# Two decode layers with a cached attention: scores in PSUM, and a larger rest of one key kept between the layers

## The chip, the core and the metric

The kernel runs on one core of a Trainium2 chip. The core has a matrix engine (TensorE, PE in the profile), a vector engine (VectorE, DVE), a scalar engine (ScalarE, ACT), a general engine (GpSimd, POOL) and a queue engine (SyncE, SP), which here only issues transfers. All of them work out of SBUF, a memory with 128 partitions; TensorE writes into a second memory, PSUM, which the kernel divides into tiles of 512 float32 columns. Sixteen DMA engines move data between the chip's main memory and SBUF. The metric is the time of one execution on the device, in microseconds (us).

## The reference

One token for each of two sequences (B = 2) goes through layer A, layer B, and then through both once more with the same weights and the same caches:

```python
def _A_ref(x, k_cache, v_cache, wq, wo):              # B=2, H=32 heads, Sk=8192 keys, Dh=128
    q = (x @ wq).reshape(B, Sq, H, Dh).transpose(0, 2, 1, 3)
    scores = einsum("bhqd,bhkd->bhqk", q, k_cache) * (Dh ** -0.5)
    p = softmax(scores)
    o = einsum("bhqk,bhkd->bhqd", p, v_cache)
    return o.transpose(0, 2, 1, 3).reshape(B, Sq, H * Dh) @ wo

def _B_ref(x, w_gate, w_up, w_down):                  # D=576, Df=4608
    return (gelu(x @ w_gate) * (x @ w_up)) @ w_down

x = A_x
for layer in range(2):
    x = x + _A_ref(layernorm(x), k_cache, v_cache, wq, wo)
    x = x + _B_ref(layernorm(x), w_gate, w_up, w_down)
```

All is float32. The two caches hold 2 x 32 x 8192 x 128 values each, 268 MB, and each layer needs all of both, against some 25 MB in the SBUF tile that the kernel loads into. So nearly all of the caches is read twice.

## The kernel before

**The work in items.** An item is a pair of heads of one sequence, or a single head. There are 30 pairs, and the heads 30 and 31 of the two sequences are four singles, s0 to s3. Layer 0 takes the 30 pairs and then s0, s1, s2, s3; layer 1 goes backward, s3, s2, s1, s0 and then the pairs. The keys of an item are laid out with 128 rows of them over the partitions and the rest along the columns. A part is 16 such rows for every partition, that is 2048 float32 columns (PART) and 1 MiB. A pair has eight parts of K and eight of V, a single four of each.

**One item on the engines.** Per unit of one or two parts, `multiply` (L578) has VectorE multiply the keys with the query, which lies repeated over the partitions in the first 128 columns of the PSUM tile qp[n % 2]; the product goes over the keys in SBUF. GpSimd adds the two halves of each row (L582). `add_up` (L588) then has VectorE sum what is left of each row into S, the scores; it is called one unit later than `multiply`, so that VectorE's order is multiply of unit k+1, sum of unit k. S is a tile of the pool `work`, which has two buffers. `peak`, `highest`, `softmax` and `total` take the maximum (L618, L625), the exponentials on ScalarE (L636, from S into `prz`, of which there are two, one for even and one for odd items) and their sum. `values` (L665) has TensorE multiply the exponentials with V, in 64 matmuls for a pair, into a PSUM tile acc. `invert`, `gather` (L680, L682: four VectorE instructions, each adding to the result of the one before) and `context` finish the item, mostly while the next is at work.

**SBUF as one tile.** `space` is one tile of END columns, and all caches and weights are loaded into it. The class `Space` decides where and when: loads stand in one list in the order of the calls of `cache`, `rows`, `out_rows`, `down` and so on. `pump` issues the first of the list as soon as its columns are free, and never a later one before it. `done` frees the columns of a part after the last instruction that reads it, and pumps again. All loads go to SP's one queue in that order, so a load that waits for its columns holds all later ones. In steady state three regions of eight parts (P0, P1, P2) take turns: the load of V goes out when VectorE has made the last sum over the keys whose place it takes, the load of K when TensorE has done the last matmul on the values whose place it takes.

**Between the layers.** What is left in SBUF at the end of layer 0 need not be read again: `kept` names four parts of K of s3 and s2, two of K of s1, and four parts of V of s1, s2, s3. For kept keys the product may not go over the keys; it goes to a `scratch` place of two parts. The MLP of layer 0 and the projections stream their weights through a ring in the middle, MID to MIDEND.

**Layer 1's start.** Its first items find their keys in SBUF. Their work is a chain on VectorE (the query's copy L604, `multiply`, `add_up`, `held_keys` L610 and L613, `gather`), while SP loads the two missing parts of K of s1, K and V of s0, and then the first pairs in several pieces.

Of the kernel before, what the change touches and what calls it, by code (L numbers as in the profile page):

```python
# [45 lines left out]
END = 24 * PART + 768  # L46
MID = 18 * PART
# [50 lines left out]


@with_exitstack  # L100
def decode_layers(ctx, tc, x_in, kc, vc, wq, wo, wg, wu, wd, out):
# [29 lines left out]
    def cache(kind, layer, item, at, lo=0, hi=None):  # L131
# [6 lines left out]
        def load(a):  # L138
            at_of[base] = a - lo * PART
            nc.sync.dma_start(space[:, a:a + (hi - lo) * PART], src[:, lo * PART:hi * PART])  # L140

        sp.queue.append(([base + (k,) for k in range(lo, hi)], at + lo * PART, (hi - lo) * PART, load))
# [88 lines left out]
    idle = {(1, NT - 2, 0): (512,), (1, NT - 2, 5): (512, 256), (1, NT - 1, 0): (160,)}  # L231
# [13 lines left out]
    scratch(s1.name, P0 + 4 * PART)  # L245
# [4 lines left out]
    cache("v", 0, s2, home[("v",) + s2.name])  # L250
# [33 lines left out]
    for k in range(2, 4):  # L284
        cache("k", 1, s1, home[("k",) + s1.name], k, k + 1)
# [38 lines left out]
    ones = consts.tile([P, P], F32, name="ones")  # L324
    nc.vector.memset(ones, 1.0)
# [11 lines left out]
    eight = consts.tile([P, 2, 4], F32, name="eight")  # L337
# [17 lines left out]
    prz = consts.tile([P, 2, 32, 2, 4], F32, name="prz")  # L355
    nc.vector.memset(prz.rearrange("p n g e r -> p (n g e r)"), 0.0)
# [3 lines left out]
    x10 = consts.tile([P, 16, 10], F32, name="x10")  # L360
# [24 lines left out]
    def turn(first=False):  # L385

        if first:
# [7 lines left out]
        stats = work.tile([P, 6], F32, name="stats")  # L395
        nc.vector.bn_stats(stats, x)
        apart = work.tile([P, B, 4, 6], F32, name="apart")
# [12 lines left out]
    def norm(apart):  # L410
# [3 lines left out]
        mv = work.tile([P, B, 2], F32, name="mv")  # L414
        for b in range(B):
            nc.vector.bn_aggr(mv[:, b, :], every[:, 24 * b:24 * b + 24])
        ve = work.tile([P, B], F32, name="ve")
# [3 lines left out]
        part = work.tile([P, 2, B], F32, name="part")  # L421
# [14 lines left out]
    def attention(layer, items, apart):  # L436
# [121 lines left out]

        def key_of(kind, item, k):
# [6 lines left out]
        def multiply(n, unit):  # L566
            item = items[n]
            lo, hi = unit
            if n not in S:
                S[n] = work.tile([P, 128], F32, name="S")  # L570
# [4 lines left out]
            if layer == 0 and lo < stays("k", item):  # L575
                at = at_of["scratch", item.name] + lo % 2 * PART
# [8 lines left out]
        def add_up(n, unit, half):  # L585
# [6 lines left out]
            n_kept = stays("k", item)  # L592
            if layer == 0 and max(0, n_kept - 2) <= lo < n_kept:
                done(("scratch", item.name, lo % 2))
# [323 lines left out]
```

## Time and profile before

The kernel took 2687.89 us, the median of three runs from 2687.64 to 2688.00 us.

| | profiled execution |
|---|---|
| time of that execution | 2687.68 us |
| its span in the trace | 2685.9 us |
| busy: VectorE | 1876.3 us, 70% |
| busy: GpSimd | 1169.2 us, 44% |
| busy: TensorE matmuls | 941.9 us, 35% |
| busy: ScalarE | 121.2 us, 5% |
| read from main memory | 1152.13 MB, 429 GB/s over the span |
| TensorE's granted clock, mean | 0.628 |

How to read it: the time of an execution is 1.78 us longer than the span, which begins and ends with the first and last recorded instruction. The span falls into stages, and times inside it count from its start: layer 0's pairs from about 30 to 1200 us, its singles to about 1270 us, the projection and the MLP of layer 0 to about 1372 us, layer 1's singles to about 1443 us, layer 1's pairs to about 2606 us, and its MLP to the end. A row of the timeline has start, duration, engine and line, and in brackets how long the engine had been idle and who ended that. Rows marked SPq are transfers being issued, not their time on the way.

### The profile page before, as it was taken

The page shows a single profiled execution, that of the slowest core. Times are in us where ns is not written, and L with a number is a line of the kernel's source. Part 1 is how long each engine was busy: PE and PEld are TensorE (multiplying, and loading weights), DVE is VectorE, ACT ScalarE, POOL GpSimd, SP SyncE. Part 2 cuts the span into 40 slices and gives each one's busy share as a digit, 9 for nine tenths or more (in the row PEclk, how much of TensorE's full clock was granted, in tenths as well). Part 3 has the DMA queues.
Part 4 walks back from the last instruction along what each step waited for, and adds up shares of the span by engine and source line. Part 5 has one row for each costly group of instructions (what it writes and reads, how often), then busy time and mean ns, then how long its engine had stood idle before and what let it go on. Part 6 is the DMA issues. An engine that isn't in the chain of part 4 may idle for free. (4 is left out here: it accounts for less than half of the span.)

```text
span 2685.9 us, 17802 instructions
## 1 busy us (share of the span) xinstructions
PE 941.9 (35%) x7226; PEld 318.8 (12%) x7226; DVE 1876.3 (70%) x1347; ACT 121.2 (5%) x542; POOL 1169.2 (44%) x341
## 2 busy tenths in 40 slices
PE   2322332233233323325764333223323332332345
PEld 0110111011001101102121111001100110110022
DVE  5578777867777787788159877776777778777750
ACT  0000000000000000001000000000000000000000
POOL 2345444544554454455025544554454445444530
PEclk7656665666566566657666666566656656665678
DMA  9999999999999999999999999999999999999998
GB/s 422 436 436 428 432 435 435 435 433 431 433 433 434 433 434 431 433 431 419 406 407 437 435 431 432 433 434 434 431 433 436 433 431 435 435 430 433 432 427 375
DMA packets 38450, 1153.29 MB, mean 429 GB/s; under 512 B 4304, under 2 KB 4960, under 8 KB 16992
## 3 DMA queue, kind: packets, MB, share of 16 engines
q1 hardware_dynamic: 38344, 1152.14, 99.8%
q8 instruction: 57, 0.93, 0.1%
q14 instruction: 25, 0.20, 0.0%
q10 hardware_dynamic: 24, 0.01, 0.0%
HBM read 1152.13 MB, written 0.00 MB: 429 GB/s over the span
## 5 line engine op out<-in xcount | busy, mean ns | idle before, releaser
L582 POOL TENSOR_TENSOR space<-space 128x2048 f32<-128x2048 f32 (+1 forms) x331 | 1165.7, 3530 | 1291.2 <-DVE space L578 1170.3
L578 DVE TENSOR_TENSOR space<-space,qp 128x4096 f32<-128x4096 f32 (+1 forms) x328 | 1126.9, 3451 | 453.9 <-DMA space<-in_A_k_cache_dram 443.5
L588 DVE TENSOR_REDUCE S<-space 128x32 f32<-128x2048 f32 (+1 forms) x331 | 594.4, 1796 | 116.7 <-POOL space L582 113.7
L665 PE MATMUL acc<-space,prz 128*8 128x512 f32 x4096 | 594.0, 743 | 9.7 <-DMA space<-in_A_v_cache_dram 5.0
L693 PE MATMUL spare<-weights,osb 128*64 128x2 f32 (+1 forms) x528 | 70.9, 256 | 1198.9 <-ACT osb L684 1180.2
L693 PEld LDWEIGHTS spare<-weights,osb 128*64 128x64 f32 (+1 forms) x528 | 65.3, 208 | 1215.5 <-ACT osb L684 1195.1
L665 PEld LDWEIGHTS acc<-space,prz 128*8 128x8 f32 x4096 | 113.0, 103 | 425.3 <-issue 419.2
L620 PE MATMUL sm<-ident,m 128*1 128x128 f32 x68 | 24.9, 367 | 335.9 <-DVE m L618 335.9
L684 ACT COPY osb<-osb 128x128 f32<-128x128 f32 x60 | 17.9, 298 | 1764.7 <-DVE osb L682 1764.7
L682 DVE SCALAR_TENSOR_TENSOR osb<-acc,diag,osb 128x128 f32<-128x128 f32 x204 | 71.6, 351 | 7.2
L419 POOL TENSOR_TENSOR rstd<-ve,mhalf 128x2 f32<-128x2 f32 x4 | 2.8, 700 | 164.0 <-DVE ve L418 164.0
L646 PE MATMUL sm<-rs,ones 128*128 128x2 f32 x120 | 35.0, 361 | 77.3 <-ACT prz L636 77.3
L636 ACT ACTIVATE prz<-S,nbs 64x128 f32<-64x128 f32 (+1 forms) x136 | 53.4, 392 | 3.1
L627 PE MATMUL sm<-m,ones 1*128 1x2 f32 (+1 forms) x136 | 39.0, 353 | 23.1 <-DVE m L625 23.1
L620 PEld LDWEIGHTS sm<-ident,m 128*1 128x1 f32 x68 | 5.4, 79 | 347.5 <-DVE m L618 317.6
L625 DVE TENSOR_REDUCE m<-sm 1x2 f32<-1x128 f32 (+1 forms) x68 | 18.9, 278 | 29.7 <-PE sm L620 29.7
L646 PEld LDWEIGHTS sm<-rs,ones 128*128 128x128 f32 x120 | 29.9, 309 | 82.4 <-ACT prz L636 82.4
L802 PE MATMUL acc<-space,xt 128*6 128x288 f32 x256 | 29.2, 568 | 29.2 <-DMA space<-in_B_w_up_dram 14.8
L813 DVE STREAM_TRANSPOSE turned<-acc 128x288 f32<-128x288 f32 x4 | 1.9, 484 | 51.8 <-PE acc L802 51.8
L627 PEld LDWEIGHTS sm<-m,ones 1*128 1x128 f32 x136 | 33.1, 300 | 41.5 <-DVE m L625 41.3
L838 PE MATMUL xps<-space,hT 128*2 128x144 f32 x576 | 32.2, 374 | 15.2 <-DMA space<-in_B_w_down_dram 15.2
L680 DVE TENSOR_SCALAR osb<-acc,diag 128x128 f32<-128x128 f32 x68 | 23.3, 342 | 15.9 <-PE acc L665 15.9
(124 smaller groups left out, 352.7 us busy)
## 6 DMA issues: line engine op xcount, KB each, us to landing
space<-in_A_k_cache_dram SPq DMA_DIRECT2D x8, 4096.0 KB, 24.7
space<-in_A_v_cache_dram SPq DMA_DIRECT2D x4, 4096.0 KB, 30.1
space<-in_B_w_down_dram SPq DMA_DIRECT2D x19, 576.0 KB, 7.3
space<-in_B_w_gate_dram SPq DMA_DIRECT2D x18, 576.0 KB, 7.5
space<-in_B_w_up_dram SPq DMA_DIRECT2D x18, 576.0 KB, 7.8
space<-in_A_wo_dram SPq DMA_DIRECT2D x16, 576.0 KB, 7.5
space<-in_A_wo_dram SPq DMA_DIRECT2D x8, 1152.0 KB, 23.7
space<-in_B_w_gate_dram SPq DMA_DIRECT2D x2, 4608.0 KB, 26.3
```

The lines of the kernel that those rows point to most:

```text
L578: nc.vector.tensor_tensor(out=u, in0=t, in1=qp_of(n)[:, 0:DH].unsqueeze(1).to_broadcast([P, j, DH]), op=ALU.mult)
L582: nc.gpsimd.tensor_tensor(out=half, in0=half, in1=u[:, :, DH // 2:], op=ALU.add)
L588: nc.vector.tensor_reduce(out=S[n][:, 16 * lo:16 * hi], in_=half, axis=AX.X, op=ALU.add)
L620: nc.tensor.transpose(peaks[n], m, ident)
L627: nc.tensor.matmul(low[n], ones[0:1, :], m1, start=True, stop=True)
L636: nc.scalar.activation(prz[rows_, n % 2, 0:item.rows // 4, e, :], s[rows_, 0:item.rows].rearrange("p (g r) -> p g r", r=4), AF.Exp, bias=n ...
L646: nc.tensor.matmul(tot, ones, rs[:, n % 2, :], start=True, stop=True)
L665: nc.tensor.matmul(acc_of(n)[32 * c:32 * c + 8, :], prz[:, n % 2, g, :, :].rearrange("p e r -> p (e r)"), space[:, at:at + 4 * DH], start= ...
L682: nc.vector.scalar_tensor_tensor(t, q[:, r, :], diag[:, r:r + 1], t, op0=ALU.mult, op1=ALU.add)
L693: nc.tensor.matmul(to[:, i, 0:item.heads], t[:, i:item.heads * DH:GH], w, start=True, stop=True,)
L802: nc.tensor.matmul(banks[half][s][32 * c:32 * c + WIN, 0:BF], lhs, space[:, lo:lo + BF], start=key not in done_first, stop=stop,)
L838: nc.tensor.matmul(xps[32 * c:32 * c + B, 0:CW], hT[t // 2][:, t % 2 * NI + i, :], space[:, a:a + CW], start=piece == downs[layer][0] and ...
```

## The change

`END` grows by MORE = 1280 columns, ten of the sixteen rows of a part. With them part 2 of K of s1 keeps its first ten rows between the layers (that is 128 x 1280 float32, 655,360 bytes), and layer 1 loads only the last six, 128 x 768. Room for it comes from smaller work tiles:

- The scores S no longer are a tile of `work` but columns 128 to 255 of the PSUM tile qp[n % 2], whose columns 0 to 127 hold the item's query (for the first item of layer 1 columns 384 to 511 of sm[1], where its query lies in the same tile).
- `prz` is single, the tile of ones [128, 128] becomes a column that is repeated by its access pattern, some small tiles share a buffer or have one buffer in place of two. The idle matmuls between the last `lower` calls are cut into pieces of 256 columns.

Since part 2 of K of s1 is kept in part, its product in layer 0 goes to a scratch place too (`more`, at P2 + 4 PART), and `shorten` then frees all but the ten rows. The scratch of s1 moves from P0 + 4 PART to P0 + 6 PART, and V of s2 in layer 0 is loaded in two halves rather than in one piece.

```diff
+MORE = 10 * DH
-END = 24 * PART + 768
-MID = 18 * PART
+END = 24 * PART + 768 + MORE
+MID = 18 * PART + MORE
...
+    def shorten(self, key, n):
+        lo, hi = self.live[key]
+        self.live[key] = lo, lo + n
+        self.pump()
...
-    def cache(kind, layer, item, at, lo=0, hi=None):
+    def cache(kind, layer, item, at, lo=0, hi=None, skip=0):
...
-            at_of[base] = a - lo * PART
-            nc.sync.dma_start(space[:, a:a + (hi - lo) * PART], src[:, lo * PART:hi * PART])
+            at_of[base] = a - skip - lo * PART
+            nc.sync.dma_start(space[:, a:a + (hi - lo) * PART - skip], src[:, lo * PART + skip:hi * PART])
...
-    idle = {(1, NT - 2, 0): (512,), (1, NT - 2, 5): (512, 256), (1, NT - 1, 0): (160,)}
+    idle = {(1, NT - 2, 0): (256, 256), (1, NT - 2, 5): (256, 256, 256), (1, NT - 1, 0): (160,)}
...
-    scratch(s1.name, P0 + 4 * PART)
+    scratch(s1.name, P0 + 6 * PART)
+    scratch("more", P2 + 4 * PART, 1)
...
-    cache("v", 0, s2, home[("v",) + s2.name])
+    for k in (0, 2):
+        cache("v", 0, s2, home[("v",) + s2.name], k, k + 2)
...
-        cache("k", 1, s1, home[("k",) + s1.name], k, k + 1)
+        cache("k", 1, s1, home[("k",) + s1.name], k, k + 1, MORE if k == 2 else 0)
...
-    prz = consts.tile([P, 2, 32, 2, 4], F32, name="prz")
+    prz = consts.tile([P, 32, 2, 4], F32, name="prz")
...
-        stats = work.tile([P, 6], F32, name="stats")
+        stats = once.tile([P, 6], F32, name="stats")
...
             if n not in S:
-                S[n] = work.tile([P, 128], F32, name="S")
+                bank, at = (sm[1], 3 * DH) if layer == 1 and n == 0 else (qp[n % 2], DH)
+                S[n] = bank[:, at:at + DH]
...
-            if layer == 0 and lo < stays("k", item):
-                at = at_of["scratch", item.name] + lo % 2 * PART
+            if layer == 0 and lo < aside(item):
+                name, k = place_of(item, lo)
+                at = at_of["scratch", name] + k * PART
...
-                if layer == 1 or k >= stays("k", item):
+                some = item is s1 and k == stays("k", item)
+                if some and layer == 0:
+                    sp.shorten(key_of("k", item, k), MORE)
+                elif layer == 1 or k >= stays("k", item):
+                    if some:
+                        sp.free(("k", 0) + item.name + (k,))
                     done(key_of("k", item, k))
...
-                    prz[rows_, n % 2, 0:item.rows // 4, e, :],
+                    prz[rows_, 0:item.rows // 4, e, :],
```

The order in which VectorE, GpSimd and ScalarE get their instructions is the same before and after. What they wait for is not, and SP's list has one load more. In the rows that follow a name ending in _49 is the counter of an engine (or, DMAHW, of a transfer) that the instruction waits for, and 128x32 is the shape of the output.

VectorE, first pair of layer 1, its first units. Here qp_124 (before) and qp_123 (after) are the PSUM tile qp of this item. Before:

```order
L578 TENSOR_TENSOR space<-space,qp_124 128x4096
L588 TENSOR_REDUCE S<-space 128x32 [waits Activation_49,Pool_49]
L578 TENSOR_TENSOR space<-space,qp_124 128x4096 [waits DMAHW1_49]
L588 TENSOR_REDUCE S<-space 128x32 [waits Pool_49]
L654 RECIPROCAL sm_127<-sm_127 128x2 [waits PE_49]
```

After:

```order
L595 TENSOR_TENSOR space<-space,qp_123 128x4096
L605 TENSOR_REDUCE qp_123<-space 128x32 [waits DVE_49,Pool_49]
L595 TENSOR_TENSOR space<-space,qp_123 128x4096 [waits DMAHW2_49,DVE_49]
L605 TENSOR_REDUCE qp_123<-space 128x32 [waits DVE_49,Pool_49]
L676 RECIPROCAL sm_126<-sm_126 128x2 [waits PE_49]
```

The sum now writes the tile that the multiply before it reads, and the multiply behind it reads the tile that the sum wrote; waits are set by tile and not by column, so each of these now waits for VectorE's own instruction ahead of it.

SP, start of layer 1, the loads of keys and values of s1 and s0. Before:

```order
L140 DMA space<-in_A_k_cache_dram 128x2048 [waits DVE_49] x2
L140 DMA space<-in_A_k_cache_dram 128x2048 [waits DMAHW0_49,DVE_49]
L140 DMA space<-in_A_k_cache_dram 128x2048 [waits DMAHW4_49,DMAHW5_49,DMAHW1_49,PE_49]
L140 DMA space<-in_A_k_cache_dram 128x2048 [waits DMAHW2_49]
L140 DMA space<-in_A_k_cache_dram 128x2048 [waits DMAHW3_49]
L140 DMA space<-in_A_v_cache_dram 128x2048 [waits PE_49] x2
```

After:

```order
L146 DMA space<-in_A_k_cache_dram 128x2048 [waits DVE_49] x2
L146 DMA space<-in_A_k_cache_dram 128x2048 [waits DMAHW1_49,DVE_49]
L146 DMA space<-in_A_k_cache_dram 128x768 [waits DMAHW5_49,DMAHW2_49,PE_49]
L146 DMA space<-in_A_k_cache_dram 128x2048 [waits DMAHW6_49,DMAHW3_49,PE_49]
L146 DMA space<-in_A_k_cache_dram 128x2048 [waits DMAHW4_49]
L146 DMA space<-in_A_v_cache_dram 128x2048 [waits PE_49] x2
```

The fourth load is smaller by ten rows; the order is the same.

SP, end of layer 0, the values of s1, s2 and s3. Before:

```order
L140 DMA space<-in_A_v_cache_dram 128x4096 [waits DMAHW5_49,DVE_49]
L140 DMA space<-in_A_v_cache_dram 128x4096 [waits DVE_49]
L140 DMA space<-in_A_v_cache_dram 128x8192 [waits DVE_49,PE_49]
L140 DMA space<-in_A_v_cache_dram 128x4096 [waits DMAHW7_49,PE_49]
L140 DMA space<-in_A_v_cache_dram 128x4096 [waits DMAHW6_49,DVE_49,PE_49]
```

After:

```order
L146 DMA space<-in_A_v_cache_dram 128x4096 [waits DMAHW5_49,DVE_49]
L146 DMA space<-in_A_v_cache_dram 128x4096 [waits DVE_49]
L146 DMA space<-in_A_v_cache_dram 128x4096 [waits PE_49]
L146 DMA space<-in_A_v_cache_dram 128x4096 [waits DVE_49]
L146 DMA space<-in_A_v_cache_dram 128x4096 [waits DMAHW7_49,DMAHW6_49,PE_49]
L146 DMA space<-in_A_v_cache_dram 128x4096 [waits DVE_49,PE_49]
```

The load of 8192 columns, which waited for TensorE and VectorE both, is now two, of which the first waits for TensorE alone.

More of the change, by code (lines that the diff above doesn't have):

```diff
@@ L557, in stays, with aside, place_of @@
             return kept.get((kind,) + item.name, 0)
+        def aside(item):
+            return stays("k", item) + (item is s1)
+        def place_of(item, lo):
+            return ("more", 0) if item is s1 and lo == 2 else (item.name, lo % 2)
         def key_of(kind, item, k):
```

52 lines of the change are left out of this document (28 added, 24 removed).

## The prediction

> **What bounds the kernel now.** I read the page first, for the engine that never rests, then the span cut into its stages, and then the handovers, the places where a load waits for work on an engine.
>
> ```profile
> span 2685.9 us, 17802 instructions
> q1 hardware_dynamic: 38344, 1152.14, 99.8%
> HBM read 1152.13 MB, written 0.00 MB: 429 GB/s over the span
> ```
>
> One queue of loads keeps the DMA engines at work for 99.8% of the span. The stages show where it is slower than it can be (columns: stretch, its length, busy time of PE, its weight loads, DVE, ACT, POOL, TensorE's granted clock, DMA share, GB/s):
>
> ```profile
> 60.00:1160.00 1100.00, 339.57 (x2268) 113.68 (x2268) 806.48 (x506) 49.21 (x224) 510.36 (x141) 0.61 1.00 433
> 1267.00:1283.00 16.00, 12.14 (x183) 5.86 (x183) 2.24 (x8) 1.05 (x5) 0.00 (x0) 0.79 0.95 365
> 1400.00:1470.00 70.00, 34.15 (x199) 11.99 (x198) 67.47 (x62) 3.75 (x19) 41.80 (x15) 0.62 1.02 434
> 1470.00:1480.00 10.00, 3.88 (x17) 1.50 (x21) 5.73 (x6) 1.15 (x5) 2.34 (x1) 0.50 1.00 419
> 1480.00:2560.00 1080.00, 337.92 (x2264) 113.44 (x2260) 801.33 (x504) 49.21 (x224) 509.90 (x140) 0.61 1.00 433
> ```
>
> 433 GB/s is the steady rate: a load of 8 MiB takes 8,388,608 / 433e3 = 19.37 us, a pair 38.7. The rate falls at layer 0's end, 1267 to 1283, and where layer 1's singles hand over to its pairs, 1470 to 1480. There the timeline shows who issues what, and when the keys land (VectorE's idle time ends with the landing):
>
> ```profile
> 1474.11 0.33 SPq L140 DMA_DIRECT2D space<-in_A_v_cache_dram  x1
> 1477.52 4.42 DVE L578 TENSOR_TENSOR space<-space,qp 128x4096 f32<-128x4096 f32 x1 [2.38 <-DMA space<-in_A_k_cache_dram]
> 1507.63 0.33 SPq L140 DMA_DIRECT2D space<-in_A_v_cache_dram  x1
> 1516.85 8.75 DVE L578 TENSOR_TENSOR space<-space,qp 128x4096 f32<-128x4096 f32 x2 [8.17 <-DMA space<-in_A_k_cache_dram]
> ```
>
> The load of V of the first pair goes out at 1474.11, only 3.4 us before the load ahead of it lands at 1477.5. Then V and the next K need 1516.85 - 1477.52 = 39.33 us where two loads take 38.7, so 0.6 us is lost here. One pair later the lead is 1516.85 - 1507.63 = 9.2 us, and VectorE, idle for 8.17 us, is far ahead. So DMA bounds the kernel, except at this handover, where VectorE's chain is nearly too late already.
>
> **The bytes saved.** The load of 128x768 in place of 128x2048 leaves out 128 x 1280 x 4 = 655,360 bytes: at 434 GB/s 1.51 us. Everything behind it in the queue could land 1.5 us earlier, the keys of 1477.52 at 1476.0. That becomes time only if the next load is issued in time. The issue at 1474.11 is SP's, and hangs on VectorE:
>
> ```profile
> SPq L140 <- DVE m L618: 46.7, 4, 22.6
> 1472.86 1.22 DVE L588 TENSOR_REDUCE S<-space 128x16 f32<-128x1024 f32 x1 [1.39 <-POOL space L582]
> DVE S L588 <- POOL space L582: 3.0, 3, 1.4
> DVE space L578 <- ACT osb L604: 2.5, 1, 2.5
> DVE m L625 <- PE sm L620: 0.8, 2, 0.5
> 1378.70 4.49 DVE L578 TENSOR_TENSOR space<-space,sm 128x2048 f32<-128x2048 f32 x2 [2.48 <-ACT osb L604]
> ```
>
> The first row is what SP waited for from 1400 to 1480, the third to fifth are all that VectorE waited for from 1378.6 to 1474.2: GpSimd's sums, the copy of the query before its first multiply, two transposes, and never a transfer. From 1378.70 to the last sum over the pair's keys, which ends at 1474.08, VectorE has one unbroken chain. No landing stands in it, so saved bytes can't shorten it. The query that starts it comes out of the MLP of layer 0, which lies ahead of the smaller load.
>
> **The waits on VectorE.** The edit of S makes a sum and its neighbouring multiplies share a PSUM tile, so VectorE waits for itself. The price, from pairs of rows with and without such a wait:
>
> ```profile
> 1453.15 2.28 DVE L588 TENSOR_REDUCE S<-space 128x32 f32<-128x2048 f32 x1
> 1455.35 4.41 DVE L578 TENSOR_TENSOR space<-space,qp 128x4096 f32<-128x4096 f32 x1
> 1467.02 1.12 DVE L682 SCALAR_TENSOR_TENSOR osb<-acc,diag,osb 128x128 f32<-128x128 f32 x3
> L682 DVE SCALAR_TENSOR_TENSOR osb<-acc,diag,osb 128x128 f32<-128x128 f32 x12 | 4.2, 351 | 0.4
> ```
>
> Without one, the multiply starts 2.20 us after a sum of 2.28: the two overlap by 0.08 us. With one, three instructions of 0.351 that each need the one before take 1.12 us, (1.12 - 3 x 0.351) / 2 = 0.034 us between them. A wait for oneself so costs 0.08 + 0.034 = 0.117 us (with the unrounded times). In the order of the changed kernel I count the rows from the first multiply of layer 1 to 1474 where an added wait is for the instruction directly ahead and no later GpSimd wait covers it: eleven sums and four multiplies, 15 x 0.117 = 1.76 us. Not counted are sums whose query lies in the other tile, and the two that stand ahead of a sum held by GpSimd (of such the 1.39 us above are one).
>
> The Trainium skill says otherwise ("VectorE: DVE Perf Modes", section "The DRAIN you can't avoid"): eight copies with a semaphore after each took the same time as with one after the last, "the semaphore costs nothing extra here". By it this term is nothing. The trace here disagrees, with 0.08 us of overlap where no wait stands and a gap of 0.034 where one does.
>
> **The scores in PSUM.** How much longer a sum takes that writes PSUM has no row; the nearest:
>
> ```profile
> L588 DVE TENSOR_REDUCE S<-space 128x16 f32<-128x1024 f32 x17 | 20.6, 1210 | 3.0 <-POOL space L582 3.0
> L588 DVE TENSOR_REDUCE S<-space 128x32 f32<-128x2048 f32 x3 | 6.8, 2281 | 0.0
> L610 DVE TENSOR_TENSOR qp<-qp,osb 128x512 f32<-128x512 f32 x1 | 0.7, 689 | 0.0
> L613 DVE TENSOR_REDUCE S<-qp 128x4 f32<-128x512 f32 x1 | 0.7, 692 | 0.0
> ```
>
> (2281 - 1210) / 1024 = 1.046 ns an element, so 512 elements would take 1210 - 535 = 675 ns out of SBUF. Out of PSUM they take 692, and into PSUM as well 689. So PSUM adds 0 to 17 ns; below nothing no row points. For 20 sums that is 0 to 0.34 us, of which I take 0.2, nearer the upper end since the two rows agree. VectorE's chain is later by 1.76 + 0.2 = 2.0 us (bounds: 0, if the waits were hidden, to 2.3, with 0.34 for PSUM and two more waits that GpSimd covers in part).
>
> **The sum at the handover.** V then goes out at 1474.1 + 2.0 = 1476.1, and the load ahead of it lands at 1476.0: the queue runs empty. How long a load takes to fill an empty queue, L, I bound from two places. At 1474.11 the lead of 3.4 us lost 0.6, so L is at most 3.4 + 0.6 = 4.0 us. At the program's start
>
> ```profile
> 0.74 0.39 SPq L140 DMA_DIRECT2D space<-in_A_k_cache_dram  x1
> 20.26 4.20 PE L449 MATMUL acc<-space,xt 128*6 128x512 f32 x24 [20.26 <-DMA space<-in_A_wq_dram]
> ```
>
> 4 MiB of K and 3 MiB of wq, 7.34 MB, have landed by 20.26; at 433 GB/s they take 16.95, and 20.26 - 16.95 - 0.74 = 2.6 us, less what of the next load had come in between, so some 2.4. The next keys then land at 1476.1 + L + 38.7 = 1514.8 + L instead of 1516.85: +0.4 us with L = 2.4, +2.0 with 4.0. I take **+1.4**, somewhat above the middle (L = 3.45), since the upper end is from this very handover. All later loads follow at the old spacing, so the shift reaches the end. The saved 1.5 us are in it: without them the load ahead would land at 1477.5, still less than L after the issue at 1476.1, and the result would be the same. The delay on VectorE eats the whole saving.
>
> **The steady pairs.** Per pair three own waits (two sums, one multiply; the others stand ahead of a GpSimd wait) and five writes to PSUM: 0.35 + 0.09 = 0.44 us on VectorE. The issue of V has 9.2 us of lead and needs at most 4.0, so it is covered; the cover ends at 5.2 us. K waits for TensorE, which gets its exponentials 0.44 us later:
>
> ```profile
> 1486.23 0.33 SPq L140 DMA_DIRECT2D space<-in_A_k_cache_dram  x1
> ```
>
> This is the tightest such issue, right behind the handover; V lands a load's 19.4 us after 1477.52, so it has 10.7 us of lead, and 0.44 is nothing beside it. That `prz` is single makes the exponentials wait until the values of the item before are done; those end at 1486 and the next exponentials come after 1507, so 20 us cover it.
>
> **The end of layer 0.** Its singles get 13 such waits, 1.5 us. VectorE there waits for values, and TensorE for the first weights of the projection:
>
> ```profile
> DVE osb L680 <- PE acc L665: 9.3, 3, 7.9
> 1264.35 0.35 DVE L680 TENSOR_SCALAR osb<-acc,diag 128x128 f32<-128x128 f32 x1 [0.89 <-PE acc L665]
> 1270.27 1.14 PE L709 MATMUL xps<-space,oT 128*2 128x144 f32 x16 [1.87 <-DMA space<-in_A_wo_dram]
> ```
>
> Two waits of `gather` for values, of which the last is 0.89 us, and 1.87 us before the projection take up more than 1.5. V of s2 in halves can go out sooner, not later, since its first half no longer waits for VectorE; it costs SP one issue of 0.33 us. So I put this at nothing; if the cover is gone, 1.5 us.
>
> **The end of the program.** The chain of layer 1's last pair is later by the same 0.44 us; its loads of weights wait for it at 2606, in a stretch where the queue is full:
>
> ```profile
> 2600.00:2612.00 12.00, 11.17 (x216) 6.31 (x208) 1.71 (x5) 0.60 (x3) 0.00 (x0) 1.00 1.04 443
> ```
>
> 443 GB/s stand there, so nothing is lost. The shared and single small tiles serve the norms and the MLP, one layer at a time, and the matmuls in pieces of 256 are idle work between loads: nothing for both.
>
> **The sum.** Layer 0 nothing, the handover +1.4, steady pairs and end nothing: 2687.68 + 1.4 = 2689.1 us for the profiled execution, and since the median of the runs is 0.2 above it, 2689.3 us. A difference of 0.2%, 5.4 us, is about what a measurement of this kernel can tell from no change; the forecast lies within it.
>
> **The rivals.**
>
> *The saving survives.* If waits for oneself cost nothing on this chain, VectorE is late by the 0.2 us of PSUM alone, V goes out at 1474.3, and the next keys land at 1474.3 + L + 38.7: with L between 2.4 and 4.0 that is -1.4 to +0.2, with 3.45 -0.4, some 2687.5 us. If VectorE isn't what the handover hangs on at all, the whole 1.5 us come out: 2686.4. For it speaks only that GpSimd's 3.0 us of waits could cover more of the added ones than I counted; against it the row of 1474.11, in which SP waits for VectorE's last sum.
>
> By the rule of the Trainium skill cited above the first half of this case would come about.
>
> *More is lost at the start of layer 1.* The query of the item after next goes into the tile that holds S, so an item's first multiply now hangs on ScalarE's exponentials of two items before. In the singles an item is four multiplies of 2.28 and four sums of 1.21, 14 us of VectorE's chain, so the exponentials are long done. Should they not be, each of the five items ahead of 1474 waits for the 0.5 us between two exponentials, 2.5 us more: +3.9, 2691.8 us.
>
> *The steady pairs lose their cover; slower by far.* Sums now write the tile from which the multiplies read the query for all their 4.41 us. If that made multiplies slower, V of every pair would go out later. A pair has three multiplies of 4.41 and two of 2.28, 17.8 us; the cover of 5.2 us, less the 0.44 already in use, is gone when they take 4.8 / 17.8 = 27% longer. From there each further 0.1 us per pair costs 0.1 x 58 = 5.8 us: slower by over 0.2% from 2693.7 us on, 2717 at 0.5 us. Against it: nothing in the rows above shows a multiply that depends on what else lies in its tile, and VectorE does one instruction after the other but for 0.08 us.
>
> *Faster by over 0.2%.* It needs 5.4 us. The saved 1.5 and all that is missing at 1267 to 1283, 16 x (1 - 365 / 433) = 2.5 us, make 4.0. So there is hardly a way.
>
> **How the numbers follow.** The forecast, saving eaten, from 2688.3 to 2690.2 us with the bounds of L and of VectorE's delay: 0.60. The saving survives, 2686.4 to 2688.1: 0.20. More lost at layer 1's start, 2690.2 to 2692.5: 0.12. Steady pairs slower: 0.06. Much faster: 0.02. The range reaches from 2686.2, the whole saving and 0.2 for the runs' spread, to 2691.2, which takes in the lower half of the third case; outside are about 0.15. The first three cases lie within 0.2% but for a hundredth of the third: within 0.2% 0.91, slower 0.07, faster 0.02.
>
> **What would show it.** In the trace of the changed kernel: sums and multiplies of layer 1's singles start 0.034 us behind the one ahead instead of 0.08 before its end; the first V of the pairs goes out near 1476 with the keys' landing near the same time; the stretch of 1470 to 1480 moves less than 405 GB/s; the distance from that landing to the next but one is over 40 us, against 39.3; the later leads stay near 9 us. It is wrong if V goes out by 1474.5, if the two landings lie under 39.4 us apart, or if a steady pair takes more than 38.8 us.

## The result, and the profile after

The changed kernel takes 2692.18 us (median of 21 runs, 2691.15 to 2693.66), the kernel before 2687.77 us (21 runs, 2686.91 to 2689.08): a ratio of 1.0017 with a 95% interval of 1.0011 to 1.0023. It is 4.4 us slower, within the 0.2% named in the prediction, and 1.0 us above the range, which ended at 2691.2. The profiled execution took 2692.31 us, 1.9 us more than its span.

The page of the changed kernel first: what is read, and who reads it.

```profile
span 2690.4 us, 18204 instructions
q1 hardware_dynamic: 38488, 1151.49, 99.6%
q14 instruction: 29, 0.24, 0.0%
HBM read 1151.47 MB, written 0.00 MB: 428 GB/s over the span
```

0.66 MB less are read, as meant, and yet the span is 4.5 us longer. 402 instructions are new, and the queue named q14 instruction carries 29 packets for 25. Where the queue is slower than before stands in the stretches (columns as in the prediction):

```profile
60.00:1160.00 1100.00, 338.04 (x2268) 113.52 (x2268) 813.85 (x506) 46.86 (x222) 510.01 (x141) 0.61 1.00 433
1267.00:1283.00 16.00, 12.22 (x159) 6.23 (x163) 3.17 (x9) 1.13 (x6) 1.05 (x1) 0.68 0.92 339
1400.00:1470.00 70.00, 33.18 (x193) 12.14 (x193) 65.95 (x58) 3.96 (x22) 40.81 (x15) 0.65 1.02 434
1470.00:1480.00 10.00, 1.56 (x11) 1.13 (x11) 8.10 (x11) 0.15 (x1) 3.39 (x2) 0.50 0.77 308
1480.00:2560.00 1080.00, 341.35 (x2266) 113.45 (x2265) 809.77 (x501) 47.17 (x224) 509.57 (x140) 0.61 1.00 433
```

It is the same two places that were slow before: the end of layer 0 (339 GB/s where 365 stood) and the handover at 1470 to 1480 (308 for 419). The steady pairs run at 433 GB/s as before. The timeline at the handover:

```profile
1379.65 4.49 DVE L595 TENSOR_TENSOR space<-space,sm 128x2048 f32<-128x2048 f32 x2 [1.79 <-ACT osb L626]
1478.33 0.33 SPq L146 DMA_DIRECT2D space<-in_A_v_cache_dram  x1
1521.08 4.42 DVE L595 TENSOR_TENSOR space<-space,qp 128x4096 f32<-128x4096 f32 x1 [10.24 <-DMA space<-in_A_k_cache_dram]
```

The first multiply of layer 1 starts 0.95 us later than before (1378.70). From it to the issue of V take 98.68 us instead of 95.41, 3.27 more. So V goes out 4.22 us later, and the next keys land 4.23 us later. The end of the span, 4.5 us later, adds little: this issue sets the time of all that follows. The load ahead of V, the keys, is issued at 1454.91; its time to landing is

```profile
DMA to landing us min/median/max: 23.1/23.1/23.1
```

so it lands at 1478.0, and the queue is empty when V goes out. From this landing to the next pass 43.1 us, where 39.33 stood. The 1.5 us of saved bytes are nowhere to be seen, and they are gone even ahead of this issue: with them the keys should land at 1476.0, and they land 0.5 us later than before the change (1477.52).

Why VectorE's chain grew by 3.27 us is read from three views of the changed kernel. Its timeline, at a sum between two multiplies and at the multiply with the longest stop ahead of it:

```profile
1423.57 2.29 DVE L595 TENSOR_TENSOR space<-space,qp 128x2048 f32<-128x2048 f32 x1 [0.40 <-issue]
...
1452.43 4.41 DVE L595 TENSOR_TENSOR space<-space,qp 128x4096 f32<-128x4096 f32 x1
1456.94 2.29 DVE L605 TENSOR_REDUCE qp<-space 128x32 f32<-128x2048 f32 x1
1459.27 4.42 DVE L595 TENSOR_TENSOR space<-space,qp 128x4096 f32<-128x4096 f32 x1
```

Its groups by shape between 1379 and 1479 (count, then busy time and the mean ns of one):

```profile
L605 DVE TENSOR_REDUCE qp<-space 128x16 f32<-128x1024 f32 x14 | 17.2, 1227 | 3.4 <-POOL space L599 2.4
L605 DVE TENSOR_REDUCE qp<-space 128x32 f32<-128x2048 f32 x3 | 6.9, 2295 | 0.3
```

Its chain of work, at the sum of 1456.94 (start, length):

```profile
1456.85 0.03 issue
1456.88 0.02 DVEq L605
1456.90 0.04 issue
1456.94 2.31 DVE qp L605
```

The multiply of 1452.43 ends at 1456.84, and the sum starts 0.10 us later; the next multiply follows the sum after 0.04 us. A sum waits for GpSimd already, and in the list of VectorE's instructions its wait for the multiply is an instruction of its own ahead of it: the chain has two pieces of issue there. So a sum's wait costs 0.083 + 0.103 = 0.186 us and a multiply's 0.117. It is not the number of waits that makes the difference: the multiply of 1459.27 waits for a transfer too, as the list of waits ahead of the prediction shows, and still follows after 0.04 us. Eleven sums and four multiplies make 11 x 0.186 + 4 x 0.117 = 2.5 us. A sum that writes PSUM takes 1227 ns for 1210 and 2295 for 2281: 20 of them 0.3 us. And one multiply, which waits for five loads and not for VectorE, starts 0.40 us after the instruction ahead has ended (1423.57); before the change it started 0.04 us before that end (1420.82), so this is 0.44 us more. Together 3.3 us. What makes that multiply stop isn't shown: with the scores alone, or with the same loads and the scores in another tile, it starts within 0.05 us of that end.

### The profile page after: what moved, and what is told of

The parts are those of the page before. It is cut to its first block, busy times and chain, and to the rows that moved or that the text cites. A ratio compares the mean times of both kernels' runs of the same rounds, so it can differ in the third digit from the quotient of the medians.

```text
span 2690.4 us, 18204 instructions
## 1 busy us (share of the span) xinstructions
PE 940.6 (35%) x7230; PEld 320.4 (12%) x7230; DVE 1896.8 (71%) x1347; ACT 116.2 (4%) x542; POOL 1169.3 (43%) x341
## 5 line engine op out<-in xcount | busy, mean ns | idle before, releaser
L605 DVE TENSOR_REDUCE qp<-space 128x32 f32<-128x2048 f32 (+1 forms) x328 | 594.8, 1813 | 122.4 <-POOL space L599 101.3
L668 PE MATMUL sm<-rs,one 128*128 128x2 f32 x120 | 34.9, 361 | 76.8 <-ACT prz L658 76.8
L658 ACT ACTIVATE prz<-qp,nbs 64x128 f32<-64x128 f32 (+1 forms) x134 | 47.8, 357 | 3.2
L649 PE MATMUL sm<-m,one 1*128 1x2 f32 (+1 forms) x136 | 39.4, 357 | 23.0 <-DVE m L647 23.0
L668 PEld LDWEIGHTS sm<-rs,one 128*128 128x128 f32 x120 | 29.7, 307 | 81.9 <-ACT prz L658 81.9
L649 PEld LDWEIGHTS sm<-m,one 1*128 1x128 f32 x136 | 33.5, 304 | 41.7 <-DVE m L647 41.5
```

The source lines that it names most:

```text
L605: nc.vector.tensor_reduce(out=S[n][:, 16 * lo:16 * hi], in_=half, axis=AX.X, op=ALU.add)
L649: nc.tensor.matmul(low[n], one[0:1, :].to_broadcast([1, P]), m1, start=True, stop=True)
L658: nc.scalar.activation(prz[rows_, 0:item.rows // 4, e, :], s[rows_, 0:item.rows].rearrange("p (g r) -> p g r", r=4), AF.Exp, bias=nbs[rows ...
L668: nc.tensor.matmul(tot, ones, rs[:, n % 2, :], start=True, stop=True)
```

## The experiments

All times are medians of eleven runs, with the kernel before timed beside them (2687.5 to 2687.9 us); the ratio's interval is about 0.0009 to either side, 2.4 us. So a difference of 1 us between two medians is no more than likely; what is read from the traces, one execution of each kernel, carries more. Only for two kernels does the ratio's interval lie wholly above 1: the scores alone, and the kernel that keeps eight rows.

**The scores alone.** S goes to PSUM in the kernel before:

```diff
-                S[n] = work.tile([P, 128], F32, name="S")
+                bank, at = (sm[1], 3 * DH) if layer == 1 and n == 0 else (qp[n % 2], DH)
+                S[n] = bank[:, at:at + DH]
```

> The kernel before with one edit: the scores lie in the PSUM tile of the query. No byte is saved, no load moved. Theory: VectorE's waits for itself delay the first V of the second pair of layer 1 from 1474.1 to about 1478 us, and this issue alone sets the time; the saved bytes were worth nothing. Then this kernel is as slow as the changed one: 2692 us (2691 to 2693). Rival, the moved and smaller loads and the small tiles are the cause: 2687.8 us. Rival, the same delay but the saved bytes had made up 1.5 us of it: 2693.5 us.

Measured: 2691.57 us, 1.0014 (1.0005 to 1.0023); V goes out at 1477.86. The edit of S by itself makes nearly the whole loss, with every byte still read. Nothing shows that the saved bytes had made up for a part of it.

**The bytes alone.** The changed kernel with `S[n] = work.tile(...)` and `MORE = 8 * DH`.

> The changed kernel with the scores back in SBUF, for which two of the ten rows are given up (eight are kept, 524,288 bytes, 1.2 us at 434 GB/s). Theory: VectorE's chain is as before, the issue stands at 1474 us again, and the saved bytes change nothing: 2687.8 us (2687.2 to 2688.5). Rival, the loads and the small tiles cost the time: 2690 us or more. Rival, the bytes come out: 2686.6 us.

Measured: 2692.38 us, 1.0017 (1.0009 to 1.0026). This was a fault of the experiment and tells nothing of either theory: with eight rows the scratch place `more`, 2048 columns, no longer fits between the keys of s1 and of s3 (768 + 1024 columns lie between), so the load of s3's keys waits for it:

```profile
1160.00:1267.00 107.00, 49.03 (x303) 16.90 (x303) 88.43 (x79) 9.12 (x37) 55.33 (x21) 0.65 0.93 399
```

399 GB/s stand where 425 stood. The ten rows are just what makes both fit (768 + 1280 = 2048).

**The bytes alone, another way**, in the kernel before, which then neither keeps nor loads these ten rows:

```diff
-            nc.sync.dma_start(space[:, a:a + (hi - lo) * PART], src[:, lo * PART:hi * PART])
+            nc.sync.dma_start(space[:, a + skip:a + (hi - lo) * PART], src[:, lo * PART + skip:hi * PART])
...
-        cache("k", 1, s1, home[("k",) + s1.name], k, k + 1)
+        cache("k", 1, s1, home[("k",) + s1.name], k, k + 1, 10 * DH if k == 2 else 0)
```

> The kernel before, with nothing changed but that the load of part 2 of K of s1 in layer 1 leaves out its first ten rows, which are not kept either: the scores of these rows are wrong, the work is the same. It shows what the saved bytes are worth with VectorE as it was. Theory, the issue of V at 1474.1 gates, with about 3.2 us from issue to a running queue: 2687.4 us (2687.0 to 2687.8). Rival, the bytes come out in full: 2686.2 us.

Measured: 2687.24 us (ratio 0.9998, 0.9989 to 1.0007). The keys ahead land 1.6 us earlier than before, the next ones do not:

```profile
1473.89 0.33 SPq L140 DMA_DIRECT2D space<-in_A_v_cache_dram  x1
1475.91 8.75 DVE L578 TENSOR_TENSOR space<-space,qp 128x4096 f32<-128x4096 f32 x2 [0.98 <-DMA space<-in_A_k_cache_dram]
1516.63 8.75 DVE L578 TENSOR_TENSOR space<-space,qp 128x4096 f32<-128x4096 f32 x2 [9.55 <-DMA space<-in_A_k_cache_dram]
```

So even with VectorE as it was the saving brings 0.4 us by the medians, a difference that the interval doesn't tell from none, and 0.2 us by the landing (1516.85 before).

**The late issue taken away.** The first sums free the first half of the place long before the last, so V of the second pair is cut into two loads:

```diff
-            if n == 0:
+            if n == 0 or (n == 1 and kind == "v"):
                 cache(kind, 1, item, at, 0, 4)
                 cache(kind, 1, item, at, 4, 8)
```

In the changed kernel:

> The changed kernel with one load cut: the V of the second pair of layer 1 goes in two halves, of which the first needs only the first four parts of the keys before it to be summed, at about 1466 us. VectorE keeps all its waits. Theory, the late issue is what costs: the queue no longer runs empty, the saved bytes come out and the 0.6 us lost at this handover before as well; the time is 2686.5 us (2685.5 to 2688). Rival, VectorE's longer work costs by itself and not through this issue: 2692 us.

Measured: 2688.64 us (1.0004, 0.9995 to 1.0013). The first half goes out at 1466.64, the keys land at 1517.46 instead of 1521.08, and 3.5 of the 4.4 us are back with all of VectorE's waits in place. That leaves the rival no room. But the expected 2686.5 was missed by 2.1 us, and most of what is missing was lost ahead of the handover: the load ahead lands at 1478.1, where the bytes alone have it at 1475.9, and 1.5 us of this lateness stand at the first multiply of layer 1 already (1380.09 for 1378.59). With the bytes left out of the kernel before:

> The same with the V of the second pair of layer 1 in two halves (the same scores are wrong). Theory: with the issue no longer late, the bytes come out in full: 2686.2 us (2685.7 to 2686.7). Rival, something else than this issue holds the time: as without the halves.

Measured: 2686.66 us (0.9996, 0.9987 to 1.0005), 0.6 us less than without the halves; the keys that landed at 1516.63 land at 1514.94. With this issue no longer late, 1.0 us comes out by the medians against the kernel before, and 1.9 us by the landing (1516.85 before): the 1.5 us of the bytes and 0.5 us that the kernel before lost at the handover itself. In the kernel before, with its bytes:

> The kernel before with the V of the second pair of layer 1 in halves, nothing else. The forecast put the 0.6 us lost at this handover down to the late issue. If so, they come out: 2687.1 us. Theory by now: 3.4 us of lead are just enough, and the 0.5 us between the two landings behind it are lost anyway: 2687.7 us (2687.3 to 2688.1), and the time from the keys' landing near 1477.5 to the next near 1516.8 stays 39.2 to 39.3 us.

Measured: 2687.98 us (1.0000, 0.9991 to 1.0009).

```profile
1478.08 8.75 DVE L578 TENSOR_TENSOR space<-space,qp 128x4096 f32<-128x4096 f32 x2 [3.40 <-DMA space<-in_A_k_cache_dram]
1516.94 8.75 DVE L578 TENSOR_TENSOR space<-space,qp 128x4096 f32<-128x4096 f32 x2 [7.70 <-DMA space<-in_A_k_cache_dram]
```

From landing to landing pass 38.86 us. The expected 39.2 to 39.3 did not come, and in the kernel before it is 39.33. In six of the kernels below, whose V has 3.8 to 4.7 us of lead, it is 38.8 to 38.9 as well. So the lead of 3.4 us did lose 0.5 us, as the forecast had it. The time of the whole is no shorter all the same, since here the load ahead lands 0.56 us later than in the kernel before (1478.08 for 1477.52). This lateness isn't the edit's: layer 0's last keys land 0.39 us later already (1171.97 for 1171.58), long ahead of the load that was cut.

**The scores in another tile** of PSUM, so that most sums and multiplies need not wait for each other:

```diff
+                if layer == 1 and n == 0:
+                    bank, at = sm[1], 3 * DH
+                elif n == last or (layer == 1 and n == 1):
+                    bank, at = qp[n % 2], DH
+                else:
+                    bank, at = xps, (2 + n % 2) * DH
```

> The changed kernel with the scores in another PSUM tile (xps) than the query, except for the first two items of layer 1 and the last item of each layer. Theory, the waits are the cost: in layer 1 ten of fifteen of them go, 1.65 us, and layer 0's end gains some 0.8 us, so the issue stands near 1476 us and the time is 2689.8 us (2689 to 2690.7). Rival, writing and reading scores in PSUM is the cost, wherever they lie: 2692 us.

Measured: 2689.93 us (1.0008, 0.9999 to 1.0017), with V at 1475.52. The scores are in PSUM as before; what went is the waits, and with them half of the loss. That went as foretold.

**The scores moved in a part of the program.** `S` goes to PSUM under a condition, else to its old tile. In layer 1 (`layer == 1`):

> The kernel before, with the scores in the query's PSUM tile in layer 1 alone. Theory: layer 0's singles, which the forecast put at nothing, delay layer 1's start by about 1 us, and the rest comes from the chain of layer 1. Then the first multiply of layer 1 starts at 1378.7 us as before, the issue of V stands near 1477.0, and the time is 2690.4 us (2689.8 to 2691). Rival, layer 0 does not matter as the forecast had it: 2691.6 us, as with the scores moved in both layers.

Measured: 2690.20 us (the ratio on record is 1.0004, 0.9993 to 1.0015; the two medians make 1.0010). The first multiply starts at 1378.68 and V goes out at 1477.01, as expected. In the pairs of both layers (all but the last of layer 0 and the first and last of layer 1):

> The kernel before with the scores in the query's PSUM tile for the pairs alone (in layer 0 all but the last, in layer 1 all but the first and the last); singles as before. It tests the step on the steady pairs. Theory and forecast: VectorE's added waits there are covered by the lead of the next load: 2687.8 us (2687.4 to 2688.2). Rival, part of the loss lies in the steady pairs: 2688.5 us or more.

Measured: 2689.59 us (1.0006, 0.9997 to 1.0015). Theory and forecast fail: by the medians pairs alone lose 1.75 us. So two runs asked whether it is what the new waits do to the stream of VectorE's instructions, in the kernel before, within `multiply` and for layer 0's pairs only:

```diff
+            if layer == 0 and n < last - 4:
+                k = item.units.index(unit)
+                nc.vector.memset(pad[:, k:k + 1], 0.0)
```

> The kernel before with five tiny instructions (a memset of one column) on VectorE in each pair of layer 0, 130 in all; nothing waits for them and no wait is added. Theory: it is the number of VectorE's instructions, whose code is fetched by transfers of 8 KB between the loads, that makes the keys of the last pair of layer 0 land at 1172.7 instead of 1171.6 us; queue 14 has 12 fetches instead of 11 from 60 to 1172 us, layer 0's end starts late, and the time is 2689 us (2688.6 to 2689.6). Rival, VectorE's waits for itself do it by the time they take: 2687.8 us and a landing at 1171.6.

Measured: 2689.36 us (1.0008, 0.9999 to 1.0017), with 13 packets on q14 up to 1172 us, where the kernel before has 11, and the last keys at 1172.35 (in a profiled execution of 2691.08 us, well above the median). By the trace's count 145 instructions were added, not 130. The other, `nc.vector.memset(xps[:, CW:512], 0.0)` once a pair:

> The kernel before with one longer instruction (a memset of 368 columns, about 0.4 us) on VectorE in each pair of layer 0, 26 in all: about as much time as the five tiny ones, but few instructions. Theory as for the run beside it: no fetch more, the landing at 1171.6 us and 2687.8 us (2687.4 to 2688.2). Rival, VectorE's time in the steady pairs counts: as slow as the scores moved for the pairs alone, 2689.6 us.

Measured: 2688.87 us (1.0004, 0.9995 to 1.0013), with 29 instructions added, 11 packets, and the last keys at 1171.97, which is as late as in kernels without any change in layer 0. If q14 were the whole cause it should have lost nothing, and by the medians it lost 1.4 us, so that theory can't explain the time. Then the edit of S in one place at a time. Layer 0's pairs, `layer == 0 and n < last - 4`:

> The kernel before with the scores in the query's PSUM tile in layer 0's pairs alone, all but the last. With the three runs beside it the edit of the scores is cut into four places. Forecast: nothing there, 2687.8 us. After the run with the pairs of both layers: the whole 1.8 us lie here, by the later landing of the last keys and what the end of layer 0 makes of it, 2689.5 us (2689.0 to 2690.0).

The end of layer 0, `layer == 0 and n >= last - 4`:

> The same in the last pair and the singles of layer 0 alone. Forecast: the 13 waits, 1.5 us, are taken up by waits for values and for the first weights of the projection: 2687.8 us. Rival, they reach the projection: the last sum of layer 0 comes 1 us or more later than at 1265.8, and the time is 2688.8 us or more.

The start of layer 1, `layer == 1 and n <= 4`:

> The same in the singles and the first pair of layer 1 alone. Theory: the chain from 1378.7 to the issue of V grows by 2.9 to 3.3 us with fifteen waits and the writes to PSUM, V goes out near 1477.2, and with 3.2 us to a running queue the time is 2690.4 us (2689.8 to 2691.0). Forecast for this term: VectorE 2.0 us later, 2689.3 us.

The pairs of layer 1, `layer == 1 and n > 4`:

> The same in the pairs of layer 1 alone, all but the first. Forecast and theory: covered by the lead of the loads, 2687.8 us (2687.4 to 2688.2). Rival, a later landing as in layer 0's pairs is worth 0.5 us or more at the end of the program too.

| scores in PSUM in | us | against before (2687.88) | last keys of layer 0 | last sum of layer 0 | V issued |
|---|---|---|---|---|---|
| nowhere | 2687.88 | | 1171.58 | 1265.77 | 1474.11 |
| layer 0's pairs | 2689.66 | +1.8 | 1173.05 | 1268.35 | 1475.50 |
| layer 0's end | 2688.76 | +0.9 | 1171.58 | 1267.07 | 1474.58 |
| layer 1's start | 2690.32 | +2.4 | 1171.84 | 1266.80 | 1476.17 |
| layer 1's pairs | 2687.56 | -0.3 | 1171.88 | 1266.86 | 1473.41 |
| all (scores alone, against 2687.70) | 2691.57 | +3.9 | 1172.74 | 1268.25 | 1477.86 |

(The times inside the span are from one profiled execution each.) By the medians the four make 4.8 us, all of them together 3.9: layer 1's start costs most, layer 0 has the rest, layer 1's pairs nothing. With the scores of layer 0's pairs moved, 1.5 us of the lateness stand at the landing of the last keys, and the rest comes at the layer's end. There weights of the projection come through a ring whose places TensorE frees one by one, and its first product waits for the softmax of s3 and for the first weights. The kernel before (its first product, at 1270.27, stands in the prediction), then layer 0's pairs alone:

```profile
1171.58 8.75 DVE L578 TENSOR_TENSOR space<-space,qp 128x4096 f32<-128x4096 f32 x2 [7.45 <-DMA space<-in_A_k_cache_dram]
1265.77 1.21 DVE L588 TENSOR_REDUCE S<-space 128x16 f32<-128x1024 f32 x1
...
1173.05 4.42 DVE L582 TENSOR_TENSOR space<-space,qp 128x4096 f32<-128x4096 f32 x1 [7.10 <-DMA space<-in_A_k_cache_dram]
1268.35 1.21 DVE L592 TENSOR_REDUCE S<-space 128x16 f32<-128x1024 f32 x1
1272.51 1.14 PE L713 MATMUL xps<-space,oT 128*2 128x144 f32 x16 [1.23 <-DMA space<-in_A_wo_dram]
```

The last sum is 2.6 us later than before, the first product 2.2 us, and the queue moves 332 GB/s at 1267 to 1283, where 365 stood. How much of such a shift is a sign? In seven kernels without a change in layer 0 the last keys land between 1171.4 and 1172.0, the last sum starts between 1265.6 and 1266.9, and the first product between 1270.3 and 1270.6. So layer 0's end alone, with its last sum at 1267.07 and the product at 1271.15, lies just outside, and its 0.9 us by the medians is within the interval.

Why the last keys of layer 0 land later stays open, but one sign separates all 18 traces. From 60 to 1172 us the queue q14 instruction carries 11 packets in twelve kernels, and their last keys land at 1171.38 to 1171.97; it carries 12 in six, and theirs land at 1172.35 to 1173.05. The kernel before, and layer 0's pairs alone:

```profile
q14 instruction: 11, 0.09, 0.0%
q14 instruction: 12, 0.10, 0.0%
```

The six are those with at least 145 more instructions on VectorE ahead of layer 1, be they waits or the five tiny ones. The scores in another tile, which lie in PSUM too but bring fewer waits, have 11 packets and 1171.56; one longer instruction has 11 and 1171.97. So the landing goes with the number of VectorE's instructions, and neither with the scores in PSUM nor with VectorE's time. That a fetch does it isn't shown: instructions and packets came together in every run, and why one packet of 8 KB more should cost 1 us is not known. Nor does it explain what the longer instruction lost.

**A better kernel.** V in halves, and S in places that no multiply reads: columns of xps, and for two singles 64 columns beside `qsb`.

```diff
+                if layer == 1 and n == 0:
+                    S[n] = sm[1][:, 3 * DH:]
+                elif item.heads == 1 and n == (last if layer == 0 else 1):
+                    S[n] = rest
+                else:
+                    bank, at = (qp[n % 2], DH) if n == last else (xps, (2 + n % 2) * DH)
+                    S[n] = bank[:, at:at + DH]
...
-        qsb = once.tile([P, CQ], F32, name="qsb", tag="row")
+        qsb = once.tile([P, CQ + 64], F32, name="qsb", tag="row")
+        qsb, rest = qsb[:, 0:CQ], qsb[:, CQ:]
```

> The changed kernel with the V of the second pair in halves and with nearly all scores out of the query's tile: in the PSUM tile xps, or, for the last single of layer 0 and the second of layer 1, in 64 columns left over beside qsb in SBUF. Theory: the waits are gone but for the first item of layer 1 and the last pair, the queue runs on, and ten rows are saved: 2686.3 us (2685.7 to 2687.0), faster than both. Rival, the small tiles or the loads of layer 0 cost something yet: 2687 to 2688 us.

Measured: 2687.29 us (0.9999, 0.9991 to 1.0008): 4.9 us better than the changed kernel, and no different from the one before that can be told. The expected 2686.3 was missed: its projection starts at 1271.55 and layer 0's end moves 352 GB/s, so some of the loss there stayed. The load ahead of the handover lands at 1478.17, no earlier than in the changed kernel, so the saved bytes are lost ahead of it here too.

## Why the prediction was wrong

**Right.** DMA bounds the kernel, the handover at 1474 hangs on VectorE, and with the delay there nothing of the saving is left. The scores alone are nearly as slow, and the bytes alone bring 0.4 us or less. The foretold signs came: under 405 GB/s at 1470 to 1480 (308), more than 40 us between the two landings (43.1), leads of the later V loads that do not shrink (11.3 us, 1509.81 to 1521.08). The rival in which the saving survives fell, since a wait for oneself costs 0.117 us or 0.186. With it fell, for this case, what the Trainium skill (VectorE: DVE Perf Modes, "The DRAIN you can't avoid") measured on eight copies, that a semaphore after each costs nothing extra.

**A rival's number by another way.** The measured 2692.2 us lies where the rival on layer 1's start had it, but that is chance. That rival had each item's first multiply wait for ScalarE's exponentials. In the changed kernel VectorE waits for ScalarE once on the way to the issue, for the copy of the query ahead of the first multiply, as before the change:

```profile
DVE space L595 <- ACT osb L626: 1.8, 1, 1.8
```

**Wrong, the size of VectorE's delay:** "VectorE's chain is later by 1.76 + 0.2 = 2.0 us". It is 3.3 in the changed kernel. Fifteen waits were right, but eleven of them stand ahead of sums that wait for GpSimd too, and there a wait costs 0.186, not 0.117: 0.8 us. The writes to PSUM took 0.3, not 0.2. The multiply held up ahead of five loads, 0.44 us, wasn't foreseen; the start of layer 1 alone, which keeps the old loads, grew by 2.9 us (first multiply at 1377.87, V at 1476.17), without it.

**Wrong, the step on layer 0's end:** "So I put this at nothing; if the cover is gone, 1.5 us." The cover was counted from the waits of `gather` and TensorE, as if each could take up the whole. TensorE's wait of 1.87 us, which was to take this up, is for a load that lies in the same queue and comes later with it. In the kernel before the first weights are issued at 1256.21 and land 14.0 us later, at 1270.2; in the changed kernel they are issued at 1259.24 and land 13.0 us later, at 1272.2:

```profile
1272.37 1.14 PE L731 MATMUL xps<-space,oT 128*2 128x144 f32 x16 [1.20 <-DMA space<-in_A_wo_dram]
```

So 1.20 us of the wait are still there, with the product 2.1 us later. Layer 0's end alone costs 0.9 us by the medians, its last sum comes 1.3 us later and the projection 0.9 us, of which up to 1.15 and 0.36 occur without any change there. So it is likely and not shown that the scores at this place cost time. But layer 0 as a whole was not nothing: in the changed kernel the first multiply of layer 1 starts 0.95 us later than before, and in the seven kernels without a change in layer 0 it is never later than before.

**Wrong, the step on the steady pairs, for layer 0:** the V loads there keep their lead, as said, and layer 1's pairs cost nothing. But in layer 0 the same edit costs 1.8 us by the medians by another way, the landing of the last keys and the end behind it. The rival on the steady pairs spoke of a lost lead and had the wrong mechanism.

**Wrong, the landing ahead:** "the load ahead of it lands at 1476.0". It lands at 1478.0, since the queue loses more in layer 0 than the saved bytes bring: the last keys there land 1.1 us later (1172.70), and 339 GB/s in place of 365 over the 16 us of its end make about 1 us more. V goes out later still, so this doesn't change the sum; it shows where V was issued in halves and 2.1 us of the expected gain did not come.

**The size of L.** From V's issue to the next keys pass 42.74 us in the kernel before and 42.75 in the changed one, and from landing to landing 38.86 where the queue doesn't run empty (the kernel before with V in halves). So L was 3.9 us in both, the upper end that the prediction had drawn from this very handover; with the start of layer 1 alone it was 3.3 (1476.17 to 1518.36). The taken 3.45 lies between, but it doesn't fit the kernel that it starts from: with it the keys of 1516.85 would land at 1474.11 + 3.45 + 38.7 = 1516.3.

The sum by these sizes: V goes out 2.2 us later than the 1476.1 of the prediction, 1.3 of it by VectorE's chain and 0.95 by layer 0, and L adds 0.6 (42.75 for 3.45 + 38.7). With the forecast's 1.4 this makes the 4.2 us that were measured. The issue was 0.5 us too late before the change already, so each further delay comes through in full.

## What to carry to other kernels

A saving in bytes is worth only what the next load's issue lets through: look for the issue with the least lead behind the place, and for the engine that sets it, before counting the bytes. Scores put into a PSUM tile from which neighbouring instructions read cost a wait in both directions here; a tile that no neighbour touches took most of these waits away. An engine's wait is cover for a delay only if what it waits for doesn't come later too. And a size taken from the middle of a range, as L was, should first give the time of the kernel that is there already.

## What was not expected of the hardware

- A VectorE instruction that waits for the one directly ahead starts 0.034 us after its end, and 0.103 us where it waits for GpSimd as well; without such a wait the two overlap by 0.08 us. A wait for a transfer beside it adds nothing at 1459.27 (0.04 us).
- Summing into PSUM costs 14 to 17 ns more than into SBUF (1227 and 2295 ns for 1210 and 2281).
- Small additions to VectorE's work in pairs that wait 7 to 8 us for DMA anyway cost 1.4 to 1.9 us by the medians, all within the intervals. Where 145 or more instructions were added the last keys of layer 0 land later, along with one packet more on the queue q14 instruction; why is open.
- A load of V issued 3.4 us ahead of the landing of the load before it lost 0.5 us; issued 3.8 us or more ahead, it lost nothing.
- The front of this text says that waits go by tile and not by column. That holds for these PSUM tiles; within the SBUF tile `space` they go by columns, as the multiply of one part and the sum of another, which do not wait for each other, show.
